# Four first PSUM tiles in another order of banks, and one root moved on ACT's queue, in a fused attention and gated feed-forward kernel

## The chip, the cores and the metric

The kernel runs on one core of one Trainium2 chip. The metric is the device time of one execution in microseconds (us); for the kernel before it is 337.18, the median of 9 runs (337.1 to 337.26). Engines: PE is TensorE (PEld its weight loads), DVE is VectorE, ACT is ScalarE, POOL is GpSimd, SP is SyncE, which only issues transfers here.

## The reference

Inputs are q, k, v of shape 8 x 8 x 576 x 64 (batch, heads, sequence, head size), a norm vector of 64, and four weight matrices. Cut to what matters:

```python
kv = np.einsum('bhsd,bhse->bhde', k, v)
out = np.einsum('bhsd,bhde->bhse', q, kv)
rms = np.sqrt(np.mean(out * out, axis=-1, keepdims=True) + 1e-06)
x = (out / rms * g_norm)          # heads side by side: x is 4608 x 512
g, val = x @ w_gate, x @ w_val    # 512 -> 1536
ffn_out = (gelu(g) * val) @ w_out # 1536 -> 512
y = x + sigmoid(x @ w_res) * ffn_out
```

The attention is linear: a 64 x 64 matrix kv for each head, then q times it, then a root-mean-square norm for each token and head.

## The kernel before

**Blocks.** A batch has 576 tokens: 512 make one block of four times 128 tokens, and the 64 that are left of all batches make a ninth block. Heads go in four pairs; the pair number is the digit in the words below. For each block the kernel makes x transposed (xT, in fp16), then 12 gate and 12 value tiles of 128 x 512 in PSUM, each with 4 matmuls on TensorE (m_gval, L365, its matmuls at L357). ACT takes the gelu of a gate tile (L345), and DVE multiplies it with the value tile (L346). Then follow the products with w_res (L377) and w_out (L394, L452) and the stores. Attention of later batches is put between these.

**The opening.** Batch 0 has nothing to hide behind, so its order on every engine is written out by hand, in a string of words, `opening` (L1041). f_piece (L990) turns each word into the instructions of one step, and each engine takes its own steps in the order of the words. For a pair p the steps are: q, k and v are cast (qc, kc, vc), q is transposed (qT), kv is made (kv) and copied out with a mask (kvo), and then

- `o`p (f_o, L927, TensorE): q times kv, 128 x 512 in one PSUM bank;
- `sq`p (L939, ACT): its squares; `rd`p (L942, DVE): their sums; `rt`p (L948, ACT): the root; `ri`p (L952, DVE): the reciprocal;
- `t`p (L956, DVE): the normalised tile; it reads the bank of `o`p for the last time;
- `xT`p (L966, TensorE): four transposes of it; `xo`p (L973 on ACT, or L971 on DVE): the copy out to xT with the norm vector;
- `g`p and `v`p (f_mm, L975, matmuls at L982, TensorE): pair p's part of the first two gate tiles and of the first two value tiles.

Pair 3 goes in two halves, a and b. The pairs come out in the order 1, 2, 0, 3. `warm` (L858) are matmuls with zeros that keep TensorE busy; `wg`, `wv` (L147) issue loads of weight columns on POOL; `wcg`, `wcv` (L1011) cast the first weight columns on POOL. `gelu` (L1052) loads ACT's function table. The four accumulating tiles of g and v are made when they are first needed:

```python
def f_mm(ws, i, pr, j0, j1):
    for f in range(2):
        if (f, i) not in tiles:
            tiles[f, i] = [pmoe.tile([P, NJ * P], FP32, tag="mm", name="gv"[i] + "ps"), 0]
```

So the word g1 takes two banks (gate tile 0, gate tile 1), and v1 the next two (value tile 0, value tile 1).

**The banks.** PSUM has 8 banks. Banks (L61) hands them out in turn: pmoe has banks 0 to 3, pattn 4 to 7. The list `opening` of pmoe is used up first: bank 0 for the tile of the warming matmuls (L854), bank 1 for o1 and bank 2 for o0 (pairs 0 and 1 take their o tiles from pmoe, in the order of the words: o1, then o0). o2 and o3 are in pattn's banks. After that the `turn` list is taken round and round, for the four tiles above and for all later gate and value tiles; at the end of block 0 banks_behind (L77) deals out the same four banks by their place in the list. A new tile in a bank waits for the last reader of the tile before it.

**Loads.** POOL issues the weights' column blocks (wg and wv 1 to 3), then w_res, the next batch's q, k and v and w_out (L1232 on), in its own order among the words.

Of the kernel before, what the change touches and what calls it, by code (L numbers as in the profile page):

```python
# [18 lines left out]
def kernel(  # L19
# [52 lines left out]
                self.turn.append(bank)  # L72
            return psum.tile(shape, dtype, tag=f"bank{bank}", name=name)

    pmoe, pattn = Banks(3, 2, 1, 0, opening=(0, 1, 2)), Banks(4, 5, 6, 7)

    def banks_behind():  # L77

# [785 lines left out]
    xT0, t0 = xT_t[0], t_t[0]  # L864
# [176 lines left out]
    opening = """  # L1041
    qc1P qc0A qT1 qT0 kc1P kc0A qo0D warm3 lk0D lv0P qo1A warm3 vc1D vc0A kv1 qc2A kv0 kvo1 kvo0 o1 kc2P qT2
    lk1P sq1 qo2D o0 warm3 warm2 vc2P sq0 lv1A rd1 kv2 qc3P rt1 kvo2 rd0 kc3A qT3 wg1 wv1 ri1 o2 rt0 t1 warm3 warm1 sq2 vc3D
    rd2 qo3A xT1 kv3 wg2 wcg0P rt2 kvo3 ri0 ri2 warm2 o3 t2 xo1A wcg1P sq3a wcv0P sq3b g1 xT2 rd3a wcv1P rd3b
    wv2 t0 xo2A wg3 wv3 v1 xT0 rt3 ri3 xo0A g2 v2 t3a t3b xT3a xT3b g0 xo3aA xo3bD gelu v0 g3a v3a g3b v3b
    """

    def first_gval():
# [221 lines left out]
```

## Time and profile before

| | before |
|---|---|
| median of 9 runs | 337.18 us |
| profiled execution, its own time | 337.1 us |
| span of that execution (first to last instruction) | 335.2 us |
| granted TensorE clock, mean | 0.995 |
| TensorE busy | 326.2 us, 97% |
| DVE busy | 253.5 us, 76% |
| ACT busy | 161.5 us, 48% |
| POOL busy | 109.2 us, 33% |
| TensorE busy between 15.70 and 17.36 us | 0.37 us of 1.66 |
| first L357 matmul (the steady stream begins) | 21.88 us |

A row in order of time gives the start in us from the span's first instruction, the duration, engine, line, operation, output<-input and how many instructions it merges; in brackets stands the idle time of the engine ahead of it and what ended that. Matmul ends are modelled: matmuls overlap, and the distance of their starts is what they cost in a row. The wait view gives, for a pair of waiter and awaited, the sum in us, the times, and the longest. A transfer's row gives the line that issued it and the time from issue to landing.

### The profile page before, as it was taken

The numbers are of one execution on the slowest core, as the hardware profiler recorded it, in microseconds if no ns is written. First come the engines' busy times: TensorE is split into PE (matmuls) and PEld (weight loads), VectorE is DVE, ScalarE is ACT, GpSimd is POOL, SyncE is SP. The second block draws the span as 40 slices with busy tenths as digits, with TensorE's granted clock in tenths as the row PEclk, the third lists the DMA queues.
The fourth block names the chain that finished last, engine by engine and source line by source line (L and its number), as shares of the span: only waits on it lengthen the run. The fifth ranks groups of instructions, "written<-read, shape, count | busy, mean of one in ns | idle before, by whom it ended". The sixth has DMA issues, their size and how long they took to land.

```text
span 335.2 us, 6522 instructions
## 1 busy us (share of the span) xinstructions
PE 326.2 (97%) x2576; PEld 200.9 (60%) x2576; DVE 253.5 (76%) x498; ACT 161.5 (48%) x290; POOL 109.2 (33%) x127
## 2 busy tenths in 40 slices
PE   8899999999999999999999999999999999999993
PEld 3444454445844485447644665467445888788872
DVE  6845449669868979798777978795789877787754
ACT  4763484274336452536173525343554375646660
POOL 2883152980065018200840066004100241142232
PEclk9999999999999999999999999999999999999998
DMA  7999999679489393965596349935200330011004
GB/s 257 315 205 203 195 203 148 171 114 140 89 128 208 74 127 127 171 58 101 160 159 63 63 127 172 120 62 96 113 0 18 62 126 2 2 63 66 0 2 125
DMA packets 76688, 38.82 MB, mean 116 GB/s; under 512 B 42098, under 2 KB 74354, under 8 KB 76658
## 3 DMA queue, kind: packets, MB, share of 16 engines
q0 software_dynamic: 38752, 17.17, 40.8%
q1 hardware_dynamic: 37328, 20.71, 23.6%
q10 hardware_dynamic: 578, 0.52, 0.5%
q8 instruction: 20, 0.33, 0.4%
q14 instruction: 10, 0.08, 0.1%
HBM read 38.80 MB, written 9.44 MB: 144 GB/s over the span
## 4 chain that ended last, share of the span: by engine, by line
PE 93%; DVE 2%; DMA 2%; SPq 1%; POOL 0%; issue 0%; ACT 0%; DVEq 0%
PE gps L357 22%; PE vps L357 21%; PE wA L452 11%; PE rps L377 9%; PE fps L394 3%; PE Av L692 3%; PE Ag L692 3%; PE wF L452 3%; PE wE L452 3%; PE wD L452 3%; PE w L452 2%; PE kvp L208 2%; PE Fg L692 2%; PE Fv L692 2%; DMA kf<-in_k_dram 2%; PE op L226 1%
## 5 line engine op out<-in xcount | busy, mean ns | idle before, releaser
L345 ACT ACTIVATE ge<-gps 128x512 f16<-128x512 f32 x84 | 50.1, 597 | 97.5 <-PE gps L357 96.7
L357 PE MATMUL gps<-xT,wg 128*128 128x512 f16 x328 | 84.3, 379 | 0.0
L357 PE MATMUL vps<-xT,wv 128*128 128x512 f16 x328 | 84.2, 379 | 0.0
L346 DVE TENSOR_TENSOR hid<-ge,vps 128x512 f16<-128x512 f16 x84 | 57.2, 682 | 32.9 <-PE vps L357 31.0
L492 POOL TENSOR_TENSOR osb<-osb,t 128x512 f32<-128x512 f32 x28 | 35.2, 1276 | 136.5 <-DVE osb L488 136.1
L357 PEld LDWEIGHTS <-wv 128*128 128x128 f16 x328 | 32.1, 98 | 38.7
L357 PEld LDWEIGHTS <-wg 128*128 128x128 f16 x328 | 30.7, 98 | 34.5 <-issue 0.2
L452 PEld LDWEIGHTS <-hid_s 128*128 128x128 f16 x384 | 37.6, 98 | 4.5 <-issue 0.2
L377 PE MATMUL rps<-wr,xT 128*128 128x512 f16 x144 | 32.5, 379 | 0.0
L452 PEld LDWEIGHTS <-hid 128*128 128x128 f16 x288 | 28.2, 98 | 5.2 <-issue 0.5
L386 ACT ACTIVATE th<-rps 128x512 f32<-128x512 f32 x36 | 21.5, 598 | 16.4 <-PE rps L377 16.4
L377 PEld LDWEIGHTS <-xT 128*128 128x128 f16 x144 | 14.1, 98 | 16.6
L245 DVE TENSOR_REDUCE ss<-sq 128x8 f32<-128x512 f32 x32 | 20.6, 679 | 2.9 <-ACT sq L243 2.7
L452 PE MATMUL wA<-wo_ts,hid_s 128*128 128x256 f16 x168 | 20.6, 273 | 0.0
L692 PEld LDWEIGHTS <-ws 128*128 128x128 f16 x192 | 18.8, 98 | 2.2
L391 ACT ACTIVATE th<-th 128x512 f32<-128x512 f32 x36 | 19.9, 622 | 0.0
L303 DVE TENSOR_TENSOR t<-op,ny 128x512 f16<-128x512 f32 x28 | 17.8, 679 | 0.1
L243 ACT ACTIVATE sq<-op 128x512 f32<-128x512 f32 x28 | 15.3, 596 | 4.5 <-PE op L226 4.2
L425 DVE TENSOR_TENSOR hid_s<-hid 128x1536 f16<-128x1536 f16 x16 | 15.3, 953 | 0.2
L317 DVE TENSOR_TENSOR t<-t,g 128x512 f16<-128x512 f16 x36 | 15.0, 461 | 0.1
L729 POOL TENSOR_TENSOR hid<-ge,c 128x512 f16<-128x512 f16 x6 | 7.0, 1163 | 23.4 <-ACT ge L723 23.4
L394 PE MATMUL fps<-wo,hid 128*128 128x512 f16 x48 | 11.2, 379 | 0.0
(173 smaller groups left out, 470.7 us busy)
## 6 DMA issues: line engine op xcount, KB each, us to landing
out_dram<-osb SPq DMA_DIRECT2D x14, 512.0 KB, 2.6
qraw<-in_q_dram POOLq DMA_DIRECT2D x7, 512.0 KB, 7.9
k<-in_k_dram POOLq DMA_DIRECT2D x7, 512.0 KB, 9.6
v<-in_v_dram POOLq DMA_DIRECT2D x7, 512.0 KB, 11.5
wg<-in_moe_w_gate_dram POOLq DMA_DIRECT2D x2, 512.0 KB, 8.7
wv<-in_moe_w_val_dram POOLq DMA_DIRECT2D x2, 512.0 KB, 9.2
wo<-in_moe_w_out_dram POOLq DMA_DIRECT2D x2, 512.0 KB, 14.0
out_dram<-osb SPq DMA_DIRECT2D x4, 256.0 KB, 2.8
```

What stands on the lines that cost most here:

```text
L245: nc.vector.tensor_reduce(out=out_, in_=sq, op=ALU.add, axis=mybir.AxisListType.X)
L303: nc.vector.tensor_tensor(out=t, in0=o, in1=scale, op=ALU.mult)
L345: nc.scalar.activation(out=ge, in_=gps, func=AF.Gelu)
L346: nc.vector.tensor_tensor(out=hids[blk][:, f, :], in0=ge, in1=vps, op=ALU.mult)
L357: nc.tensor.matmul(ps[:, j0 * P : j1 * P], lhsT=w[:, cc, :], rhs=xT_t[blk][:, j0:j1, cc, :], start=(cc == 0 and j0 == 0), stop=(cc == NP - ...
L377: nc.tensor.matmul(rps, lhsT=xT_t[blk][:, j, cc, :], rhs=wr16[:, cc, :], start=(cc == 0), stop=(cc == NP - 1),)
L386: nc.scalar.activation(out=th, in_=rps, func=AF.Tanh, scale=0.5)
L391: nc.scalar.activation(out=th, in_=th, func=AF.Copy, scale=0.5, bias=0.5)
L394: nc.tensor.matmul(fps, lhsT=hids[blk][:, f, j * P : (j + 1) * P], rhs=wo16[:, f, :], start=(f == 0), stop=(f == NF - 1))
L452: nc.tensor.matmul(ps[:, e - es[0], :], lhsT=a[:, f, e * P : (e + 1) * P], rhs=b[:, f, :], start=(start and e == es[0] and f == 0), stop=( ...
L492: nc.gpsimd.tensor_tensor(out=res_all[of], in0=res_all[of], in1=t_t[blk][of], op=ALU.add)
L692: nc.tensor.matmul(out_[:, r, :], lhsT=lhsT, rhs=rhs, start=(first and r == 0 and c == 0), stop=(c == 1), skip_group_check=True,)
```

## The change

Two edits, both in what the opening uses. First, the turn list of pmoe is 3, 1, 0, 2 instead of 3, 2, 1, 0. Second, the word rt3 (the root of pair 3, on ACT) stands ahead of xo2A (the copy of pair 2's transposes, on ACT) instead of behind xT0.

```diff
-    pmoe, pattn = Banks(3, 2, 1, 0, opening=(0, 1, 2)), Banks(4, 5, 6, 7)
+    pmoe, pattn = Banks(3, 1, 0, 2, opening=(0, 1, 2)), Banks(4, 5, 6, 7)
...
-    wv2 t0 xo2A wg3 wv3 v1 xT0 rt3 ri3 xo0A g2 v2 t3a t3b xT3a xT3b g0 xo3aA xo3bD gelu v0 g3a v3a g3b v3b
+    wv2 t0 rt3 xo2A wg3 wv3 v1 xT0 ri3 xo0A g2 v2 t3a t3b xT3a xT3b g0 xo3aA xo3bD gelu v0 g3a v3a g3b v3b
```

No instruction is added or removed. The order on TensorE, DVE, POOL and SP is the same as before; on ACT the two instructions rt3 and xo2 change places. Ahead of these words, the opening has `g1 xT2 rd3a wcv1P rd3b`.

| tile | bank before, held until then by | bank after, held until then by |
|---|---|---|
| gate 0 (g1) | 3, new | 3, new |
| gate 1 (g1) | 2, o0 | 1, o1 |
| value 0 (v1) | 1, o1 | 0, warming matmuls |
| value 1 (v1) | 0, warming matmuls | 2, o0 |

## The prediction

> **What bounds the kernel now.** I read three views of the profile in this order: the page's first rows and its chain of work that ended last, then TensorE's waits, then the order of time between 14 and 22 us, engine by engine.
>
> ```profile
> PE 326.2 (97%) x2576; PEld 200.9 (60%) x2576; DVE 253.5 (76%) x498; ACT 161.5 (48%) x290; POOL 109.2 (33%) x127
> PE 93%; DVE 2%; DMA 2%; SPq 1%; POOL 0%; issue 0%; ACT 0%; DVEq 0%
> ```
>
> TensorE is busy 97% of the span and holds 93% of the chain. So a microsecond in which TensorE stands still in the opening is a microsecond of the result, unless a transfer with a fixed landing time catches it later. Of TensorE's waits, this is the longest:
>
> ```profile
> PE gps L982 <- DVE t L956: 1.3, 1, 1.3
> ```
>
> It is one wait, of L982 (the first gate matmuls) for L956 (the normalising multiply). TensorE in order of time:
>
> ```profile
> 15.69 0.38 PE L982 MATMUL gps<-xT,wg 128*128 128x512 f16 x1 [0.24 <-ACT xT L973]
> 17.36 0.38 PE L982 MATMUL gps<-xT,wg 128*128 128x512 f16 x1 [1.29 <-DVE t L956]
> 17.57 0.39 PE L966 MATMUL xtp<-ident,t 128*128 128x128 f16 x4
> 17.79 0.59 PE L982 MATMUL vps<-xT,wv 128*128 128x512 f16 x2
> 18.22 0.39 PE L966 MATMUL xtp<-ident,t 128*128 128x128 f16 x4
> 18.73 0.59 PE L982 MATMUL gps<-xT,wg 128*128 128x512 f16 x2
> 19.16 0.59 PE L982 MATMUL vps<-xT,wv 128*128 128x512 f16 x2
> 19.69 0.61 PE L966 MATMUL xtp<-ident,t 128*128 128x128 f16 x4
> 20.14 0.59 PE L982 MATMUL gps<-xT,wg 128*128 128x512 f16 x2
> ...
> 21.88 0.59 PE L357 MATMUL gps<-xT,wg 128*128 128x512 f16 x2
> ```
>
> In program words the rows are g1 (its two matmuls stand apart), xT2, v1, xT0, g2, v2, xT3a with xT3b, g0 and so on; 21.88 is where the steady stream begins. DVE and ACT beside it:
>
> ```profile
> 15.33 0.69 DVE L956 TENSOR_TENSOR t<-op,rinv 128x512 f16<-128x512 f32 x1
> 15.96 0.75 DVE L942 TENSOR_REDUCE ss<-sq 128x4 f32<-128x256 f32 x2
> 16.62 0.68 DVE L956 TENSOR_TENSOR t<-op,rinv 128x512 f16<-128x512 f32 x1
> 18.90 0.20 DVE L952 RECIPROCAL rinv<-rms 128x8 f32<-128x8 f32 x1 [1.60 <-ACT rms L948]
> 19.21 0.75 DVE L956 TENSOR_TENSOR t<-op,rinv 128x256 f16<-128x256 f32 x2
> ```
>
> ```profile
> 15.54 0.66 ACT L939 ACTIVATE sq<-op 128x256 f32<-128x256 f32 x2
> 17.99 0.69 ACT L973 ACTIVATE xT<-xtp,gcol 128x512 f16<-128x512 f16 x1 [1.79 <-PE xtp L966]
> 18.58 0.29 ACT L948 ACTIVATE rms<-ss,eps_col 128x8 f32<-128x8 f32 x1
> 18.77 0.68 ACT L973 ACTIVATE xT<-xtp,gcol 128x512 f16<-128x512 f16 x1
> ```
>
> DVE's rows are t2 (ends 16.02), rd3a and rd3b (end 16.71), t0 (ends 17.30), ri3, t3a and t3b. ACT's are sq3a and sq3b, xo2, rt3, xo0. The second matmul of g1 takes bank 2, which holds o0, and o0's last reader is t0. So g1 stalls until 17.36, and xT2, queued behind it, stalls too, although its own input t2 was there at 16.02. Behind xT2 wait xo2, and on ACT's queue behind xo2 the root rt3, whose input was there at 16.71; DVE then sits 1.60 us until rt3.
>
> **Part 1, the banks.** Four allocations change banks: gate tile 0 stays in 3, gate tile 1 goes from 2 to 1, value tile 0 from 1 to 0, value tile 1 from 0 to 2. Bank 1 held o1, whose last reader t1 is over before 14 us. Bank 0 held the warming matmuls, TensorE's own. So g1 and v1's first matmul lose the wait, and v1's second matmul gets it. What is queued behind that one on TensorE is xT0, which reads t0 itself and could not start earlier; who waits for xT0 is xo0, then g0. TensorE until the wait: g1 at 15.69 and 15.91 (0.215 each, from 17.36 to 17.57); xT2 about 0.05 after t2 ends (as 17.36 follows 17.30), at 16.08, its result at 16.47 (0.39); v1's first matmul once the weight cast on POOL is through, and even if it waited for both casts they end before t0:
>
> ```profile
> 16.04 1.18 POOL L1011 CAST wv<-wvf 128x512 f16<-128x512 f32 x2 [0.33 <-DMA wvf<-in_moe_w_val_dram]
> ```
>
> 16.04 + 1.18 = 17.22. So all three are issued before 17.36. From 17.36 TensorE has left: v1's second matmul 0.21, xT0 0.22 (17.57 to 17.79), g2 and v2 0.86 (four of 0.215), xT3a and b 0.22, and what ran from 20.14 to 21.88 without a stall, 1.74. Sum 3.25, end at **20.61 instead of 21.88: 1.27 us less**. The other way round: 0.65 of matmuls moves ahead of 17.36, and stalls of 0.62 behind it go (0.29 between 18.44 and 18.73, for xo2; 0.33 within 19.59 to 20.14, for t3a and t3b). The stall up to 17.36 itself stays, though shorter.
>
> **Part 2, the root.** rt3 goes ahead of xo2 on ACT. It can start 0.03 after rd3b, 16.74, and holds xo2, whose input is there at 16.47, until 16.93 (rt3 and the copy behind it, 18.58 and 18.77 above, are 0.19 apart). That is a wait added: behind it stand xo2, xo0, xo3a. xo2 ends at 16.93 + 0.69 = 17.62, and g2 wants it at 17.79: 0.17 of cover. With the old order xo2 would end about 17.2. ri3 comes right behind t0, 17.22 to 17.42; t3a starts 0.31 after ri3 as before, 17.53; t3b ends at 18.28, where xT3b wants it at 18.76. With the banks alone, rt3 would start about 17.1 and t3b end about 18.48, still 0.28 early. So **part 2 adds nothing to part 1** (cost 0; without the covers named, at most 0.2 either way). Alone, with the old banks, it would take away the 0.33 before g0: end at 21.55.
>
> **Does TensorE itself then bound the rest?** xT0's result is out at 17.74 + 0.22 = 17.96, xo0 runs 17.99 to 18.67, g0 wants it at 18.87: cover 0.15, the thinnest. xo3a runs 18.97 to 19.44 for 19.73. The table load follows, 19.46 to 20.74 (1.28 in its row), and the first gelu runs 20.75 to 21.35; its bank is wanted again at 20.61 + 8 x 0.215 = 22.33. All hidden.
>
> A rule speaks against this last point: the Trainium skill, page "ScalarE: Activation LUTs", section "What ACT_TABLE_LOAD costs", charges every switch with a drain of about 1.38 us besides the load. In this trace the load starts 0.02 behind the last copy and the gelu 0.01 behind the load, so the drain is not seen; by the rule the first gelu would end at 22.73 and the third gate tile would be held 0.4, leaving 0.8 of the gain. I go by the rows.
>
> **What is late next** is a transfer. Issues on POOL do not move. The tightest is the third value block, issued at 17.16:
>
> ```profile
> wv<-in_moe_w_val_dram POOLq DMA_DIRECT2D x1, 512.0 KB, 7.4
> ```
>
> It lands at 24.6. The fifth value tile's matmuls start at 26.20 and would start at 24.93 (their first weight load 0.1 earlier): 0.2 to 0.3 is left. The output weights' third block (issued 32.45, 14.2 to landing: 46.6) is needed at 48.48, then at 47.2: 0.6 left. The batch-1 values and keys' remainder have more. From 58 us on the queue has drained and every load follows the work. So I count nothing for landings. Blocks of 512 KB land 2.5 to 3.0 us apart in this stretch, so a landing may move by 0.5; less the margin of 0.2 to 0.3 it costs 0 to 0.3, and I keep 0.5 for the range, since two such landings may add up. Later allocations only rename banks: each bank passes to the tile with the same part as before.
>
> **Sum.** Profiled execution: 337.1, of which 335.2 is the span. 335.2 - 1.27 = 333.9 and 335.8. The median of the nine runs, 337.18, lies 0.1 above the profiled run, so I say **335.9**.
>
> **Rivals.**
> 1. A landing or a copy on ACT is late next and takes part of it. For: covers of 0.15 to 0.3 are thin, and the queue is saturated until 58 us. Against: all are positive in the one execution seen. With 0.3 to 0.9 taken back: 336.2 to 336.8. Chance 0.12.
> 2. The wait only changes place: something I don't see (v1's first matmul in the warming bank, or xo2 behind rt3) keeps TensorE until the same time, and only the 0.33 or less remains: 336.9 to 337.2. For: t0 ends at 17.30 in any case. Against: only v1's second matmul and xT0 need it. Chance 0.05.
> 3. Slower: TensorE's clock drops in the opening. At the start warming matmuls follow each other at 0.43 (weight loads at 1.59, 2.02, 2.44 and still 6.93, 7.36), then 0.215. If the stop before 17.36 brought that state back for as long as it took at first (6.4 us), half of it, 3.2, would be lost: 337.2 - 1.3 + 3.2 = 339.1. It decides from a stop longer than 1.29, and the row at 17.36 shows 0.215 right after such a stop. The new stops are about 0.2 and 0.3. Chance 0.03.
>
> Page "TensorE: Matmul & The Clock Gate", section "A second HAM failure mode: psum-queue depth-cycling", says that micro-idling between bank-cycling groups can throttle repeatedly; the granted clock is 1.00 from 14 to 58 us here. With a window of 3.4 us at half rate (that page's Part 1), an estimate, 1.7 would be lost and the sum would be 0.4 slower; the rows give no loss.
>
> **The numbers.** Forecast 0.80. About 0.2%, 0.67 us, is what measurement can tell from no change. Faster by more: the forecast and most of rival 1, 0.88; within, from the rest of rival 1 and most of rival 2: 0.08; slower, rival 3 and a little of rival 2: 0.04. The range reaches from 335.6 (0.3 for run to run and a slack I missed) to 336.5, where the landings' bound of 0.5 is used up.
>
> **What would show it.** In the new profile: xT2 near 16.1; L982 for a value tile waiting for L956 until 17.36, some 0.3; rt3 at 16.74 and xo2 at 16.93; no stall between 17.36 and the first L357 matmul, that one at 20.6; the stream behind it without a wait for wv. Wrong if that matmul comes at 20.6 and the span shrinks by less than 1, or if a stall for xo0, xo2 or a transfer stands in between.

## The result, and the profile after

| | before | after |
|---|---|---|
| median | 337.18 us (29 runs) | 335.88 us (9 runs) |
| ratio, 95% interval | | 0.9965 (0.9956 to 0.9973) |
| profiled execution / its span | 337.1 / 335.2 us | 335.88 / 333.9 us |
| first L357 matmul | 21.88 us | 20.63 us |

The change takes 1.3 us away, 0.35%, clear of the interval. The executions of the kernel before and of the changed one, and less cleanly those of most others here, fall into a lower group and one some 0.65 us above it (335.82 to 335.90 and 336.45 to 336.66 after; 337.1 to 337.4 and 337.65 to 338.1 before), for which the last section gives a reason in the first 10 us, and where a difference is below 0.5 us I compare the medians of the lower groups, 337.17 before and 335.87 after.

The first row of the page, and the two waits of TensorE that now stand in the place of the one of 1.3 us:

```profile
PE 325.7 (98%) x2576; PEld 200.8 (60%) x2576; DVE 253.3 (76%) x498; ACT 161.5 (48%) x290; POOL 109.2 (33%) x127
```

```profile
PE vps L982 <- DVE t L956: 0.3, 1, 0.3
...
PE vps L982 <- POOL wv L1011: 0.2, 1, 0.2
```

The waiter is now a value tile (vps), no longer a gate tile, and it waits 0.3. TensorE in order of time, from g1 on:

```profile
15.70 0.59 PE L982 MATMUL gps<-xT,wg 128*128 128x512 f16 x2 [0.24 <-ACT xT L973]
16.13 0.39 PE L966 MATMUL xtp<-ident,t 128*128 128x128 f16 x4
16.72 0.39 PE L982 MATMUL vps<-xT,wv 128*128 128x512 f16 x1 [0.21 <-POOL wv L1011]
17.37 0.38 PE L982 MATMUL vps<-xT,wv 128*128 128x512 f16 x1 [0.26 <-DVE t L956]
17.58 0.38 PE L966 MATMUL xtp<-ident,t 128*128 128x128 f16 x4
...
20.63 1.03 PE L357 MATMUL gps<-xT,wg 128*128 128x512 f16 x4
```

Both matmuls of g1 stand together at 15.70, xT2 follows at 16.13 instead of 17.57, v1's first matmul waits for its weight cast, its second for t0. From 17.37 to the steady stream nothing is idle: 3.26 us. On ACT the root comes first, and on DVE ri3 no longer waits:

```profile
16.75 0.30 ACT L948 ACTIVATE rms<-ss,eps_col 128x8 f32<-128x8 f32 x1 [0.54 <-DVE ss L942]
16.96 0.67 ACT L973 ACTIVATE xT<-xtp,gcol 128x512 f16<-128x512 f16 x1
```

```profile
17.23 0.20 DVE L952 RECIPROCAL rinv<-rms 128x8 f32<-128x8 f32 x1
17.53 0.75 DVE L956 TENSOR_TENSOR t<-op,rinv 128x256 f16<-128x256 f32 x2
```

From the first L357 matmul to the last matmul of the program, each starts 1.25 or 1.26 us earlier than its mate in the kernel before: nothing is given back on the way.

### The profile page after: what moved, and what is told of

Same layout as the page of the kernel before. It is cut to its first block, busy times and chain, and to the rows that moved or that the text cites. A ratio compares the mean times of both kernels' runs of the same rounds, so it can differ in the third digit from the quotient of the medians.

```text
span 333.9 us, 6522 instructions
## 1 busy us (share of the span) xinstructions
PE 325.7 (98%) x2576; PEld 200.8 (60%) x2576; DVE 253.3 (76%) x498; ACT 161.5 (48%) x290; POOL 109.2 (33%) x127
## 4 chain that ended last, share of the span: by engine, by line
PE 93%; DVE 2%; DMA 2%; SPq 1%; POOL 0%; issue 0%; DVEq 0%
PE gps L357 22%; PE vps L357 21%; PE wA L452 11%; PE rps L377 9%; PE fps L394 3%; PE Av L692 3%; PE Ag L692 3%; PE wF L452 3%; PE wE L452 3%; PE wD L452 3%; PE w L452 2%; PE kvp L208 2%; PE Fg L692 2%; PE Fv L692 2%; DMA kf<-in_k_dram 2%; PE op L226 1%
## 5 line engine op out<-in xcount | busy, mean ns | idle before, releaser
L357 PE MATMUL gps<-xT,wg 128*128 128x512 f16 x328 | 84.3, 380 | 0.0
L357 PE MATMUL vps<-xT,wv 128*128 128x512 f16 x328 | 84.2, 379 | 0.0
L357 PEld LDWEIGHTS <-wv 128*128 128x128 f16 x328 | 32.1, 98 | 38.7
L357 PEld LDWEIGHTS <-wg 128*128 128x128 f16 x328 | 30.7, 98 | 34.5 <-issue 0.2
L692 PEld LDWEIGHTS <-ws 128*128 128x128 f16 x192 | 18.8, 98 | 2.2
```

The lines of the kernel that those rows point to most:

```text
L357: nc.tensor.matmul(ps[:, j0 * P : j1 * P], lhsT=w[:, cc, :], rhs=xT_t[blk][:, j0:j1, cc, :], start=(cc == 0 and j0 == 0), stop=(cc == NP - ...
L692: nc.tensor.matmul(out_[:, r, :], lhsT=lhsT, rhs=rhs, start=(first and r == 0 and c == 0), stop=(c == 1), skip_group_check=True,)
```

## The experiments

My theory: the gain is the place that the tile behind o0 has in TensorE's queue. Whatever is queued there or behind it waits for t0, TensorE bounds everything after that, and the root's place matters only as far as a cover of a few tenths reaches. The rivals: the root is what pays; TensorE is not the bound; the transfers decide.

### The banks alone

```diff
-    pmoe, pattn = Banks(3, 2, 1, 0, opening=(0, 1, 2)), Banks(4, 5, 6, 7)
+    pmoe, pattn = Banks(3, 1, 0, 2, opening=(0, 1, 2)), Banks(4, 5, 6, 7)
```

> The new order of banks, with rt3 left between xT0 and xo0 as before. My theory (the wait of g1 for bank 2 is the whole of it, and the root is then early enough in either place): the same as the changed kernel, 335.9 us; the first L357 matmul at 20.63, xo2 at 16.55 and rt3 about 17.15 on ACT, the last half of t3 done at 18.5 with 0.2 to 0.3 to spare. Rival (the root's move is needed for part of the gain, because DVE's chain rt3, ri3, t3 is late next): TensorE stops ahead of xT3, 336.1 to 336.6 us.

Measured: 335.94 us (335.88 to 336.38), ratio to before 0.9962 (0.9948 to 0.9975), lower group 335.92. ACT's copy comes first here and the root behind it:

```profile
16.61 0.69 ACT L973 ACTIVATE xT<-xtp,gcol 128x512 f16<-128x512 f16 x1 [0.34 <-PE xtp L966]
17.20 0.29 ACT L948 ACTIVATE rms<-ss,eps_col 128x8 f32<-128x8 f32 x1
```

This execution starts g1 0.06 later, at 15.76, and reaches the first L357 matmul at 20.69: 4.93 us, as after (15.70 to 20.63). The banks are the whole gain; the rival, that DVE's chain from the root would be late, does not hold.

### The root alone

```diff
-    wv2 t0 xo2A wg3 wv3 v1 xT0 rt3 ri3 xo0A g2
+    wv2 t0 rt3 xo2A wg3 wv3 v1 xT0 ri3 xo0A g2
```

> The banks as before, rt3 ahead of xo2. My theory: g1 still waits for t0 until 17.36, only the 0.33 us of stalls around xT3 goes; the first L357 matmul at 21.55, 336.85 us. Rival (the root pays most of the gain): below 336.4 us. Rival (the root pays nothing even alone): 337.2 us.

Measured: 337.23 us (336.86 to 337.57), ratio 0.9996 (0.9987 to 1.0005), which by itself tells nothing from no change: five of the 11 runs lie at 337.52 to 337.57 and one, 337.23, between the groups; the lower five, 336.86 to 336.96, have the median 336.89. The profiled execution is one that started late (g1 at 16.41, 0.7 us later than before), so I read it by differences:

```profile
18.09 0.38 PE L982 MATMUL gps<-xT,wg 128*128 128x512 f16 x1 [1.30 <-DVE t L956]
...
22.28 0.38 PE L357 MATMUL gps<-xT,wg 128*128 128x512 f16 x1
```

The wait of 1.30 is there as before. From its end to the steady stream it takes 4.19 us, before 21.88 - 17.36 = 4.52: the 0.33 that the prediction gives for the root alone.

### Value tile 0 behind o0

```diff
-    pmoe, pattn = Banks(3, 1, 0, 2, opening=(0, 1, 2)), Banks(4, 5, 6, 7)
+    pmoe, pattn = Banks(3, 1, 2, 0, opening=(0, 1, 2)), Banks(4, 5, 6, 7)
```

> As the changed kernel, but the banks in the order 3, 1, 2, 0, so that value tile 0 instead of value tile 1 follows o0 in bank 2. My theory: one more matmul of 0.215 us stays behind t0, the first L357 matmul at 20.84, 336.1 us. Rival (TensorE is not what bounds the stretch from 17.36 to the steady stream): no change from 335.9 us.

Measured: 336.21 us (336.09 to 336.80), ratio 0.9972 (0.9963 to 0.9981), lower group 336.16, so 0.29 above the changed kernel where one matmul of 0.215 was expected. In the profile both matmuls of v1 start from 17.43, and the first L357 matmul is at 20.91, 3.48 later, against 3.26 after: the 0.22 of one matmul. The other 0.07 is as much as this execution was late at g1 (15.77 instead of 15.70). TensorE bounds this stretch.

### The root one place later, behind xo0, with the new banks

```diff
-    wv2 t0 xo2A wg3 wv3 v1 xT0 rt3 ri3 xo0A g2
+    wv2 t0 xo2A wg3 wv3 v1 xT0 xo0A rt3 ri3 g2
```

> The new banks, but rt3 one place later than before, behind xo0 on ACT. My theory (the root's place has a cover of 0.2 to 0.3 us with the new banks and no more): rt3 at 18.6, the halves of t3 end at 19.65 and 20.0, TensorE stops ahead of both halves of xT3, the first L357 matmul at 21.9, 337.2 us: the whole gain is lost. Rival (the root's place does not matter at all once the banks are right): 335.9 us.

Measured: 337.69 us (337.17 to 337.83), ratio 1.0004 (0.9995 to 1.0013), lower group 337.19: the gain is gone, as my theory said. TensorE now stops ahead of xT3, and from v1's second matmul to the steady stream it takes 4.52 us instead of 3.26:

```profile
19.89 0.61 PE L966 MATMUL xtp<-ident,t 128*128 128x128 f16 x4 [0.88 <-DVE t L956]
```

So the root's place is free from ahead of xo2 to between xo2 and xo0, and one place further it costs 1.3 us.

### Gate tile 0 behind o0

```diff
-    pmoe, pattn = Banks(3, 1, 0, 2, opening=(0, 1, 2)), Banks(4, 5, 6, 7)
+    pmoe, pattn = Banks(2, 3, 1, 0, opening=(0, 1, 2)), Banks(4, 5, 6, 7)
```

> As the changed kernel (root early), but the banks in the order 2, 3, 1, 0, so that gate tile 0, the very first, follows o0 in bank 2. My theory (each matmul that stands behind t0 on TensorE's queue is paid, and xT2 behind them pays its copy too): both matmuls of g1, xT2 and v1 start at 17.36 or later, g2 then waits for xo2 until 18.93, the first L357 matmul at 21.75, 337.05 us where the runs' lower group is meant. Rival (only the 1.29 us wait counts, wherever it stands): the same as with gate tile 1 in bank 2 and the root early, 336.9 us.

Measured: 338.50 us (337.26 to 338.68), ratio 1.0025 (1.0015 to 1.0035): slower than before, and both expectations missed. Eight of the twelve runs lie at 338.47 to 338.68, the profiled one among them; the other four, 337.26 to 337.86, are 0.2 to 0.8 above the 337.05 expected. TensorE in order of time, and its clock by stretches (the stretch and its length; busy time of TensorE, its weight loads, DVE, ACT and POOL, each with its number of instructions; the granted clock; the DMA engines' share and GB/s):

```profile
17.52 0.59 PE L982 MATMUL gps<-xT,wg 128*128 128x512 f16 x2 [2.00 <-DVE rinv L952]
...
19.12 1.01 PE L982 MATMUL gps<-xT,wg 128*128 128x512 f16 x2
19.92 1.06 PE L982 MATMUL vps<-xT,wv 128*128 128x512 f16 x2
```

```profile
17.50:19.10 1.60, 1.51 (x12) 0.90 (x13) 0.75 (x2) 0.72 (x2) 1.60 (x3) 0.91 1.30 206
19.10:22.50 3.40, 3.38 (x12) 1.54 (x12) 0.35 (x1) 1.90 (x3) 3.40 (x5) 0.54 1.24 208
```

The waits are those expected (g1, xT2 and v1 behind t0, g2 at 19.12 behind xo2; the profile names ri3 as g1's releaser, which ends 0.03 before it; t0, the last reader of bank 2, ends at 17.38, just ahead). What I had not expected of this kernel is the clock: TensorE stood for 2.0 us, and then it is granted 0.91 and 0.54. Two matmuls of 512 columns take 0.80 and more from start to start instead of 0.43. By these two rows the half rate lasted 2 x (0.09 x 1.60 + 0.46 x 3.40) = 3.4 us. It did not begin with the stop's end: 0.09 x 1.60 lost ahead of 19.10 is 0.3 us at half rate, so, as an estimate, the fall came near 18.8, 1.3 us after TensorE had started again and 3.3 us after the stop began (15.5).

### The same with warming matmuls in the stop

```diff
-    rd2 qo3A xT1 kv3 wg2 wcg0P rt2 kvo3 ri0 ri2 warm2 o3 t2 xo1A wcg1P sq3a wcv0P sq3b g1 xT2
+    rd2 qo3A xT1 kv3 wg2 wcg0P rt2 kvo3 ri0 ri2 warm2 o3 t2 xo1A wcg1P sq3a wcv0P sq3b warm3 warm3 g1 xT2
```

> Gate tile 0 in bank 2 and the root early as in the run that lost most, but with six more warming matmuls ahead of g1, so that TensorE does not stand for 2.0 us. Theory (the extra loss there, 338.5 us where 337.05 was worked out from the waits, is TensorE's clock, granted at half for 3.4 us after the long stop): the six matmuls run from 15.4 to 16.7, the clock stays at 1.00, matmuls of 512 columns stay 0.215 us apart, the first L357 matmul comes at 21.8 to 21.9 instead of 23.46, and the time is 337.0 to 337.2 us (upper group 337.7). Rival (the clock has nothing to do with the stop): about 338.5 us as without them, or more, since six matmuls are added.

Measured: 337.15 us (337.07 to 337.77), ratio 0.9999 (0.9990 to 1.0008), lower group 337.12. With six useless matmuls added the kernel is 1.35 us faster. The two were timed on different chips, with the kernel before at 337.26 and 337.16 us beside them, so the chip accounts for 0.1 of it. The stop is 0.7 us instead of 2.0, and the clock stays whole:

```profile
15.50:17.50 2.00, 1.29 (x7) 0.43 (x6) 1.96 (x5) 1.05 (x4) 1.65 (x4) 1.00 1.45 197
...
19.10:22.50 3.40, 3.40 (x23) 2.06 (x23) 0.35 (x1) 2.80 (x4) 3.40 (x5) 1.00 1.23 205
```

The first L357 matmul is at 21.90 and the time within 0.1 of the 337.05 worked out from the waits alone. So the extra loss of the run before is the clock after a long stop, shown by shortening the stop. The Trainium skill, page "TensorE: Matmul & The Clock Gate", section "What's actually happening", lets the clock fall after at least one idle window of about 3.4 us. Here a stop of 2.0 us was enough for it, in the profile and, by their times, in eight of the twelve runs, while its length of 3.4 us at half rate agrees; after stops of 1.3 us, as in the kernel before, the profiles show none.

### A fifth bank

Value tile 1 takes a free bank of the other pool, which gets bank 2 for the first half of xT3; the banks are new, and the root is in its old place.

```diff
             if (f, i) not in tiles:
+                if (f, i) == (1, 1):
+                    pmoe.turn[0], pattn.turn[:2] = pattn.turn[0], [pattn.turn[1], pmoe.turn[0]]
```

> The new order of banks, rt3 in its old place, and value tile 1 in a bank of the other pool that is free at that time; bank 2 goes to that pool in exchange, as the first half of xT3. No tile of g1 or v1 then follows o0. My theory (one matmul of 0.215 us still stands behind t0 in the changed kernel): the first L357 matmul at 20.42 to 20.45 instead of 20.63, 335.7 us; TensorE's wait for t0 stays, on xT0. Rival (xT0, xo0 or the halves of t3 are late next, their covers being 0 to 0.2 us): no gain, 335.9 us.

Measured: 336.01 us (335.84 to 336.36), ratio 0.9964 (0.9952 to 0.9975), lower group 335.86: not told apart from the changed kernel by time. The profile shows the step itself:

```profile
16.73 0.61 PE L984 MATMUL vps<-xT,wv 128*128 128x512 f16 x2
17.55 0.40 PE L966 MATMUL xtp<-ident,t 128*128 128x128 f16 x4 [0.21 <-DVE t L956]
```

Both matmuls of v1 are ahead of the wait, which has moved to xT0. From g1 (15.87) to the first L357 matmul (20.61) it takes 4.74 us, 0.19 less than after; but this execution starts g1 0.17 later, and so the time does not show it. In the profile of the same kernel with fewer warming matmuls, below, it takes 4.74 again (16.05 to 20.79).

### A late landing, before and after

The issues of the third value block and the fourth gate block change places on POOL, in the kernel before and in the changed one.

```diff
-    wv2 t0 xo2A wg3 wv3 v1
+    t0 xo2A wg3 wv2 wv3 v1
```

> The kernel before, with the issues of the third value block and the fourth gate block exchanged on POOL, so that the third value block lands where the other did, at 26.6 to 27.1 us instead of 24.1 to 24.6. The fifth value tile is then late by 0.4 to 0.9 us: 337.6 to 338.1 us. Theories agree on this one; it is the mate of the next.

> The changed kernel with the same exchange. My theory (a landing does not move with the work, so a late one takes the gain back): the fifth value tile waits 1.7 to 2.2 us instead of 0.4 to 0.9, and the kernel ends within 0.1 us of its mate, 337.6 to 338.1 us. Rival (the transfers follow the work, so that the gain is kept): 1.25 us below its mate, 336.4 to 336.9 us.

Measured: 337.81 us (337.63 to 338.90), ratio 1.0018 (1.0010 to 1.0027), from the kernel before, and 338.08 us (337.85 to 340.0), ratio 1.0033 (1.0017 to 1.0048), from the changed one. TensorE's wait for the block, before and then after:

```profile
PE vps L357 <- DMA wv<-in_moe_w_val_dram: 0.3, 1, 0.3
```

```profile
PE vps L357 <- DMA wv<-in_moe_w_val_dram: 1.2, 1, 1.2
```

The fifth value tile starts at 26.73 in the one and 26.95 in the other, right after the landing, and the spans are 335.7 and 335.9: the landing sets the end, and the 1.25 us are gone. (In the profile of the second the opening itself was 0.66 late; without that it would have waited 1.2 + 0.66, some 1.9, an estimate.) My theory is right in that; that the two would agree within 0.1 was too narrow, since landings of the same issue differ by some tenths between executions. Four of the second kernel's ten runs are at 338.66 to 340.0, and one of the first's eleven at 338.90. TensorE's stop there may bring the half rate back, but none of these runs was profiled, so that is open.

### Fewer warming matmuls

```diff
-    qc1P qc0A qT1 qT0 kc1P kc0A qo0D warm3 lk0D lv0P qo1A warm3 vc1D vc0A kv1
+    qc1P qc0A qT1 qT0 kc1P kc0A qo0D warm3 lk0D lv0P qo1A warm1 vc1D vc0A kv1
```

> The changed kernel with two of the warming matmuls ahead of the first kv product left out (one word of three becomes one). Theory (the runs' upper group, 0.65 us above the lower, are executions in which TensorE runs its first matmuls at half rate for longer, so that the warming matmuls hold up the first kv): the upper group comes down, from 336.5 to 336.0 to 336.2 us, and the lower stays at 335.9. Rival (fewer warming matmuls make TensorE's slow start longer): the upper group gets more frequent or later, 336.5 us and above.

> The kernel with the fifth bank and the root in its old place, with the same two warming matmuls left out. Theory: as the run before this one, less one matmul of 0.215 us behind t0, 335.7 us in the lower group. Rival (nothing is left to gain there, since the start of the opening varies by more): 335.9 us.

> The changed kernel itself, as the mate of the other two on the same chip: 335.9 us in the lower group, 336.5 in the upper.

Measured on the same chip: 335.85 us (335.81 to 335.97), ratio 0.9954 (0.9941 to 0.9968); 335.80 us (335.64 to 336.0), ratio 0.9952 (0.9940 to 0.9965); and the changed kernel again 335.91 us (335.85 to 336.51), ratio 0.9960 (0.9948 to 0.9973). Without the two warming matmuls none of the ten runs is in the upper group, and the fifth bank gives the lowest times of all, 335.64 and 335.69, 0.2 below the changed kernel's lowest. In both profiles the first kv product now waits for the cast of v on DVE (0.41 and 0.44 us), and no longer for the warming matmuls. But the changed kernel itself has one run of five in the upper group here, and with five runs each the intervals overlap: both times point the way my theory says, and neither is shown.

## Why the prediction was right

Step by step, as the prediction put it and as the profile after has it:

| step | predicted | measured |
|---|---|---|
| g1's two matmuls | 15.69, 15.91 | 15.70, 15.91 |
| xT2 | 16.08 | 16.13 |
| v1's second matmul, behind t0 | 17.36 | 17.37 |
| rt3, xo2 | 16.74, 16.93 | 16.75, 16.96 |
| ri3, t3a | 17.22, 17.53 | 17.23, 17.53 |
| first L357 matmul | 20.61 | 20.63 |
| span; median | 333.9; 335.9 | 333.9; 335.88 |

- **Part 1, 1.27 us.** Measured 1.25. That the banks alone give it is shown by the first experiment, and that each matmul left behind t0 costs its 0.215 by value tile 0 in bank 2.
- **Part 2, nothing beside part 1 and 0.33 alone.** Both shown: 335.92 with the banks alone, and 0.33 in the stretch with the root alone. The covers were real: one place later and the whole 1.3 us is lost. On ACT, xo2 ended 0.17 ahead of g2 (17.63 and 17.80), as predicted, and xo0 0.20 ahead of g0 (18.69 and 18.89), where the prediction had 0.15 and called it the thinnest.
- **Table load.** It started 0.02 us behind the last copy (19.47, after 18.98 + 0.47), and the gelu at 20.77, right behind its 1.28 us. No drain was paid that would hold TensorE, as the row before had it. (The tile that a drain would have held is the fourth gate tile, not the third: the third gate and value tiles take two banks of the other pool, and so the first gelu's bank is wanted again only at 22.35.)
- **Landings, counted at nothing.** The third value block landed somewhat earlier in this execution:

```profile
wv<-in_moe_w_val_dram POOLq DMA_DIRECT2D x1, 512.0 KB, 6.9
```

  17.16 + 6.9 = 24.1, and it was wanted at 24.94: 0.8 of cover, where the prediction had 0.2 to 0.3 from the landing at 24.6. That the landing came 0.5 earlier is luck, which the forecast did not need: the 0.2 to 0.3 would have been enough. So rival 1 had a true mechanism that did not come into play; the late landing shows what it would have cost.
- **Rival 2**, the wait only changing its place, holds for 0.26 us of it, on v1's second matmul, as part 1 had counted. The fifth bank moves that wait on to xT0 and keeps 0.19 of it.
- **Rival 3**, the clock. The mechanism exists in this opening, and the point was rightly put beyond a stop of 1.29 us: it came at 2.0, and where between the two it lies is open. Its price was wrong: 3.2 us was taken from the first 7 us of the program, and a fall in mid-program lasted 3.4 us and cost 1.4 by the times (338.50 against 337.12) and 1.5 by the two profiles (the first L357 matmul 5.94 and 4.41 us after g1).

## What to carry to other kernels

When tiles take buffers in turn, ask for each whose last reader it waits for and what is queued behind it on the in-order engine: give the buffer that comes free last to the tile that stands last in that queue, best beside work that waits for the same thing anyway. On an engine that bounds the rest, the gain is the work that can move ahead of the wait plus the stalls that the late work caused, and it reaches the end only as far as the next landing has cover. A second edit that shortens a chain is worth nothing where the first has already given that chain slack; test it alone before it is credited.

## What the runs showed of the hardware

- A stop of TensorE of 2.0 us cost more than itself: 3.4 us at half rate, which by the estimate above began only 1.3 us after the stop's end; eight of twelve runs were that much slower, and six dummy matmuls in the stop took it away. Stops of 1.3 us did not do it in the two profiles that have them (the kernel before, the root alone).
- The upper group of run times fits a late start of the opening, by some 0.7 us, which comes from TensorE's first microseconds. The same six warming matmuls and, for the second, the first kv product, in the kernel before and in the execution profiled with the root alone:

```profile
6.51 2.03 PE L858 MATMUL idle<-zeros 128*128 128x512 f16 x6
```

```profile
6.50 2.77 PE L858 MATMUL idle<-zeros 128*128 128x512 f16 x6
9.06 0.63 PE L916 MATMUL kvp<-v,k 128*128 128x128 f16 x4
```

  In the first, the matmuls go from 0.43 to 0.215 us apart near 7.6, and the first kv product starts at 8.51. In the second all six are 0.43 apart, the first kv product starts at 9.06, its four matmuls are 0.11 apart instead of 0.055, and g1 starts at 16.41 instead of 15.69. It is the kv products at half rate that go with the late g1, and not the late start of the first: with the fifth bank that one starts at 9.07 too, but goes over to full rate with its second matmul,

```profile
9.07 0.42 PE L916 MATMUL kvp<-v,k 128*128 128x128 f16 x4
```

  and g1 starts at 15.87, in a run of the lower group (335.84). Of the profiles here only the one with the root alone and the one of the changed kernel with the late landing have those four matmuls at half rate (a row of 0.63), and of all in which the first matmul of g1 does not wait for t0 only these two start it 0.66 to 0.72 late. No run of the changed kernel's own upper group was profiled; that its upper runs have the same cause is argued from the size alone. The same page and section of the Trainium skill say that the window is free-running, so that the time of the change varies from run to run; the profiles agree, with changes near 7.6 and near 9.7. The granted clock is shown as 1.00 in both throughout this stretch, although the matmuls are 0.43 apart, so here the distance of the starts is the better witness.
- A transfer issued at the same time landed at 24.1 in one execution and 24.6 in another. Covers of a few tenths are within that.
